# The plan of an attention kernel begins with VectorE and ScalarE still busy, and six small row transfers change their queue

## The chip, the cores and the metric

The kernel runs on one core of a Trainium2 chip. The metric is device time in microseconds (us) of one execution; the time before is the median of three. TensorE (PE in the profile) multiplies, VectorE (DVE), ScalarE (ACT) and GpSimd (POOL) work elementwise, SyncE (SP) issues most DMAs; ScalarE can issue DMAs from its own queue too.

## The reference

The input x has 2048 rows of 1024. Layer normalisation gives xn; an attention of 32 heads of 32 columns and a dense layer pair with Mish between (3584 wide) both read xn, and the output joins them.

```python
xn = _layernorm(x, axis=-1)
s = _A_ref(xn, A_wqkv, A_wo)
g = _silu(_B_ref(xn, B_w1, B_b1, B_w2))
return x + s * g
...
scores = jnp.einsum("bhqd,bhkd->bhqk", q, k) * (Dh ** -0.5)
p = _softmax(scores, axis=-1)
o = jnp.einsum("bhqk,bhkd->bhqd", p, v)
```

Everything is fp32. Products are made from a rounded high part and a low part each (three matmuls for one), which is why the code speaks of high and low, or of `THREE`.

## The kernel before, in words

There are four stages. In the first, x is normalised and transposed, and v is made for all heads. In the second ("qk"), 16 groups of 128 columns of q and k are made, four tiles of 512 rows each (`qk_group`, L626 is its matmul, in 24 steps); each tile leaves through ScalarE (high part), VectorE (low part) and a store issued from ScalarE's queue. The third is the plan, described below. The fourth finishes the output projection and writes the result.

Softmax needs the maximum of each row of scores before the exponentials. The kernel makes scores twice. First come the s tiles (queries on partitions, 128 by 512): VectorE takes the maximum of each (`mx`). Of 16 query tiles the 64 maxima go through a chain: reduce over the four key chunks and negate (`nm`), split into high and low (`hl`), turn by TensorE (`mtp`), copy by ScalarE (`mt`), and then two DMAs write them as rows 96 and 97 into the head's `qstack`, the right operand of the second pass. In the second pass the t tiles (keys on partitions, 512 queries each) come out with the maximum subtracted already, and ScalarE writes exp of them into `p`. A t tile of column block c (c = 0 to 3), called t(c=0) and so on, reads the 512 query columns of block c, rows 96 and 97 among them. GpSimd adds the p tiles up for the sum (`z`), TensorE multiplies them by v (`pv`).

For head 0, the s tiles and the first three quarters of the chain run already in the last four groups of the qk stage: `s_mm` (L553 matmul, L557 maximum) and, for every four query tiles, `m_tail` (groups g = 0, 1, 2, which become column blocks c = 0, 1, 2). The steps of `m_tail` are not issued at once but after 1, 2, 9 and 10 ticks of `Later`, a list that is run at the end of each tile and emptied when the stage ends. Group 0's rows so go out in the last qk tiles, those of groups 1 and 2 at the very end. The last four query tiles' maxima are finished inside the plan, by `m_chain(0, 12, 4, ...)`, and t(c=3) of head 0 waits for it (`m_there[0, 3]`); t(c=0) to t(c=2) of head 0 have no such entry in the planner's needs. The semaphores hold the real order in any case.

Within one engine's queue, instructions go in the order of the program. In the third stage that order is written by a planner (`Plan`, run once when the program is built). Five streams offer TensorE work: s of the next heads (L702), t (L785) with pv (L832), h (the first dense layer, L933, 24 matmuls for one tile), y (the second dense layer, L1022), and the output projection (L1119). Each matmul has a due time (`key`); the other engines' operations are added as their inputs are offered. The planner keeps a clock for each engine (`self.at`), gives each operation a fixed duration from the code, and takes from what is ready the one with the lowest key. Things that are limited are rings: seven PSUM banks `b`, two s tiles (`S_B`), two t tiles (`T_B`), and so on; an operation that takes from a ring waits, in the planner's time, until a place is given back. The planner's time decides only the order; the chip then runs it as semaphores allow.

All clocks of the planner begin at 0. The banks, which the qk stage still uses when the plan begins, have start times of their own:

```python
plan.rings["b"] = [(t, i) for i, t in enumerate((0.0, 0.2, 0.3, 0.9, 1.5, 2.1, 2.7))]
```

A DMA goes to SyncE's queue unless an engine is given:

```python
def move(out_, in_, eng=None):

    (eng or nc.sync).dma_start(out_.bitcast(F32), in_.bitcast(F32))
```

Of the kernel before, what the change touches and what calls it, by code (L numbers as in the profile page):

```python
# [18 lines left out]
P = 128  # L19
# [194 lines left out]
def body(ctx: ExitStack, tc: tile.TileContext, x, wqkv, wo, w1, b1, w2, out):  # L214
    nc = tc.nc
# [54 lines left out]
    def copy(out_, in_, scale=1.0):  # L270
        nc.scalar.activation(out_, in_, AF.Copy, scale=scale)  # L271

    def move(out_, in_, eng=None):

        (eng or nc.sync).dma_start(out_.bitcast(F32), in_.bitcast(F32))

    def low(eng, out_, in_, high):

        eng.tensor_tensor(out_, in_, high.bitcast(F32), ALU.subtract)  # L279
# [246 lines left out]
    def parts(i, n):  # L526
        return hls[i][:, :2 * n].rearrange("p (a b) -> p a b", a=2)

    def turn(tp, i):
        nc.tensor.matmul(tp[:, :P], hls[i], ident_r, start=True, stop=True)  # L530
# [30 lines left out]
    def m_tail(h, g, mx):  # L561
        nm = early.tile([P, NT], F32, tag=f"nm{g % 2}", name=f"nm{h}_{g}")[:, :4]
        hl = parts(g % 2, 4)
        mt = sp.tile([8, P], F32R, tag="mt", name=f"mt{h}_{g}")

        def r1():
            nc.vector.tensor_reduce(nm, mx[:, :4], axis=AX.X, op=ALU.max, negate=True)

        def r2():
            copy(hl[:, 0], nm)  # L570
            low(nc.vector, hl[:, 1], nm, hl[:, 0])

        def r3():
            tp = ps1.tile([P, 512], F32, tag="ps", name=f"mtp{h}_{g}")
            turn(tp, g % 2)
            copy(mt, tp[:8, :P])

        def r4():
            for a in range(2):
                move(qst[h % 3][96 + a:97 + a, g * 512:(g + 1) * 512]  # L580
                     .rearrange("o (t p) -> o t p", p=P), mt[4 * a:4 * a + 4, :])

        for t, fn in ((1, r1), (2, r2), (9, r3), (10, r4)):
            later.at(t, fn)
# [81 lines left out]
    plan = Plan()  # L666
# [6 lines left out]
    for i in (7, 6, 3, 1, 4, 2, 0, 5):  # L673
        ps_a.tile([P, 512], F32, tag=f"b{i}", name=f"free{i}")
    plan.rings["b"] = [(t, i) for i, t in enumerate((0.0, 0.2, 0.3, 0.9, 1.5, 2.1, 2.7))]

    def bank(at, name):
        return ps_a.tile([P, 512], F32, tag=f"b{at['b']}", name=name)
# [547 lines left out]
    for c in range(NC):  # L1226
        for s in range(4):
            t = 4 * c + s
# [49 lines left out]
```

## Time and profile before

| what | before |
|---|---|
| median of three runs | 3424.2 us (3423.58 to 3424.74) |
| the profiled execution's own time | 3424.24 us |
| its span in the trace | 3422.0 us |
| TensorE busy in the span | 3398.7 us |
| SyncE's queue, `qstack<-mt` issues in the whole span | 70 |

The span runs from the first to the last instruction of the program; the execution's own time is 2.2 us longer. Times in the trace are counted from the start of the span; the plan's first matmul is the s matmul at 577.53. A row of a timeline gives start, length, engine and line, what is written and read, how many instructions are merged into the row, and in brackets how long the engine stood idle ahead of it and what ended that. A q behind the engine's name (ACTq, SPq) is its queue issuing a DMA. Matmuls overlap, so that one that takes 0.39 us follows another 0.227 us later.

### The profile page before, as it was taken

Reading aid. Unit: us, or ns where it says so; the run is one execution under the profiler, and the core shown is the slowest. Engines: PE = TensorE matmul, PEld = TensorE weight load, DVE = VectorE, ACT = ScalarE, POOL = GpSimd, SP = SyncE. Lnnn points to the kernel's source line nnn. Section 1 sums busy time; section 2 is a strip of 40 time slices with the busy share of each in tenths; the row PEclk is TensorE's granted clock in tenths of the full one; section 3 lists DMA queues with packets and bytes.
Section 4 is the critical chain, followed back from the end, with each engine's and each line's share of the span. In section 5 each row is a group of like instructions: output and inputs, shape, how many; then the busy total and the mean of one; then the engine's idle time right before and its main releaser. Section 6 shows DMA issues by size and latency. Waiting matters only on the chain.

```text
span 3422.0 us, 47293 instructions
## 1 busy us (share of the span) xinstructions
PE 3398.7 (99%) x17827; PEld 2535.1 (74%) x17827; DVE 2326.9 (68%) x3750; ACT 1948.0 (57%) x3112; POOL 2461.5 (72%) x753
## 2 busy tenths in 40 slices
PE   8999999999999999999999999999999999999999
PEld 8998887677777767777677777777777677777687
DVE  6011236877878777788878787877878788876533
ACT  6111112766666667666666676666666666666621
POOL 0654342988888888888888888888888888888700
PEclk9999999999999999999999999999999999999999
DMA  8898897433334354343434443333445443333482
GB/s 289 288 309 303 292 314 241 124 111 100 118 105 124 105 167 136 111 120 103 124 99 124 149 148 111 112 117 107 126 113 183 123 121 112 112 117 119 140 290 85
DMA packets 294184, 529.71 MB, mean 155 GB/s; under 512 B 88810, under 2 KB 147178, under 8 KB 270186
## 3 DMA queue, kind: packets, MB, share of 16 engines
q1 hardware_dynamic: 274100, 484.74, 45.8%
q10 hardware_dynamic: 19856, 41.95, 3.3%
q8 instruction: 141, 2.31, 0.3%
q14 instruction: 87, 0.71, 0.1%
HBM read 386.89 MB, written 138.67 MB: 154 GB/s over the span
## 4 chain that ended last, share of the span: by engine, by line
PE 97%; DVE 2%; ACT 1%; DMA 0%; issue 0%; POOL 0%; DVEq 0%; POOLq 0%; ACTq 0%
PE y L1022 18%; PE h L933 17%; PE t L785 13%; PE pv L832 13%; PE s L702 13%; PE qk L626 10%; PE op L1119 5%; PE v L328 5%; DVE mx L708 1%; PE zp L858 1%; PE s L553 0%; PE pt L383 0%; ACT p L268 0%; DMA vraw<-in_A_wqkv_dram 0%; DVE st L355 0%
## 5 line engine op out<-in xcount | busy, mean ns | idle before, releaser
L814 POOL TENSOR_TENSOR z<-z,p 128x2048 f32<-128x2048 f32 x448 | 2066.2, 4612 | 192.0 <-ACT p L268 163.0
L268 ACT ACTIVATE p<-t,zero 128x512 f32<-128x512 f32 x2048 | 1385.3, 690 | 637.8 <-PE t L785 621.8
L708 DVE TENSOR_REDUCE mx<-s 128x1 f32<-128x512 f32 x1984 | 1327.8, 685 | 436.9 <-PE s L702 429.0
L1022 PE MATMUL y<-w,act 128*128 128x512 f32 x2688 | 937.7, 391 | 0.6 <-DVE yacc L1042 0.5
L785 PE MATMUL t<-qstack,kstack 128*128 128x512 f32 x2048 | 801.6, 393 | 0.9 <-DVE mx L708 0.6
L702 PE MATMUL s<-kstack,qstack 128*128 128x512 f32 x1984 | 779.4, 394 | 3.8 <-DVE mx L708 3.4
L933 PE MATMUL h<-xr,w 128*128 128x512 f32 x2016 | 715.2, 392 | 1.8 <-ACT act L271 1.8
L1022 PEld LDWEIGHTS y<-w,act 128*128 128x128 f32 x2688 | 503.0, 188 | 118.2 <-issue 8.4
L785 PEld LDWEIGHTS t<-qstack,kstack 128*128 128x128 f32 x2048 | 384.1, 188 | 110.4 <-issue 16.8
L702 PEld LDWEIGHTS s<-kstack,qstack 128*128 128x128 f32 x1984 | 371.3, 188 | 126.1 <-issue 24.3
L832 PE MATMUL pv<-p,v 128*32 128x512 f32 x4096 | 459.3, 594 | 0.0
L933 PEld LDWEIGHTS h<-xr,w 128*128 128x128 f32 x2016 | 378.9, 188 | 85.4 <-issue 5.0
L626 PE MATMUL qk<-xc,qkw 128*128 128x512 f32 x1536 | 350.9, 389 | 0.0
L814 POOL TENSOR_TENSOR z<-p,p 128x2048 f32<-128x2048 f32 x32 | 148.0, 4624 | 263.2 <-ACT p L268 182.2
L832 PEld LDWEIGHTS pv<-p,v 128*32 128x32 f32 x4096 | 123.3, 110 | 282.8 <-issue 282.1
L626 PEld LDWEIGHTS qk<-xc,qkw 128*128 128x128 f32 x1536 | 288.2, 188 | 59.8
L1042 DVE TENSOR_TENSOR yacc<-yacc,y 128x512 f32<-128x512 f32 x416 | 282.6, 679 | 52.3 <-PE y L1022 51.4
L933 PE MATMUL h<-xc,w 128*128 128x512 f32 x672 | 242.4, 391 | 0.1
L279 DVE TENSOR_TENSOR qst<-qk,qst 128x512 fp32r<-128x512 f32 x64 | 44.2, 691 | 246.0 <-ACT qst L271 246.0
L271 ACT ACTIVATE qst<-qk 128x512 fp32r<-128x512 f32 x64 | 38.3, 598 | 298.4 <-PE qk L626 262.1
L328 PE MATMUL v<-vw,xc 128*128 128x256 f32 x1536 | 191.1, 285 | 2.5 <-POOL vw L279 1.5
L328 PEld LDWEIGHTS v<-vw,xc 128*128 128x128 f32 x1536 | 186.9, 193 | 4.1 <-POOL vw L279 1.9
(91 smaller groups left out, 2273.7 us busy)
## 6 DMA issues: line engine op xcount, KB each, us to landing
w<-w1s SPq DMA_DIRECT2D x112, 1024.0 KB
w<-w2s SPq DMA_DIRECT2D x224, 512.0 KB
w2s<-pw SPq DMA_DIRECT2D x56, 512.0 KB
qstack<-qs SPq DMA_DIRECT2D x96, 256.0 KB
kstack<-ks SPq DMA_DIRECT2D x96, 256.0 KB
w1s<-w1p SPq DMA_DIRECT2D x20, 1024.0 KB
praw<-in_B_w_dram SPq DMA_DIRECT2D x72, 256.0 KB
x<-in_A_x_dram SPq DMA_DIRECT2D x32, 512.0 KB
```

The lines of the kernel that those rows point to most:

```text
L268: nc.scalar.activation(out_, in_, fn, bias=zero if bias is None else bias, scale=scale)
L328: nc.tensor.matmul(ps[:, :256], xc[t // 4][k // HK][:, a, k % HK, (t % 4) * P:(t % 4 + 1) * P], w[:, b, k], start=n == 0, stop=n == 3 * KT ...
L626: nc.tensor.matmul(ps, w[:, a, k], xc[c][k // HK][:, b, k % HK], start=n == 0, stop=n == 3 * KT - 1)
L702: nc.tensor.matmul(sp_, qst[h % 3][:, qt * P:(qt + 1) * P], kst[h % 3][:, kc * 512:(kc + 1) * 512], start=True, stop=True)
L708: nc.vector.reduce_max(tiles["mx"][:, qt, kc:kc + 1], tiles[qt, kc], axis=AX.X)
L785: nc.tensor.matmul(tp, kst[h % 3][:, kt * P:(kt + 1) * P], qst[h % 3][:, c * 512:(c + 1) * 512], start=True, stop=True)
L814: nc.gpsimd.tensor_tensor(zs[h], pts[T - 1] if kt == 1 else zs[h], pts[T], ALU.add)
L832: nc.tensor.matmul(pv[h][c * DH:(c + 1) * DH, :], vt[h][:, k, :], pts[T - kt + k][:, c * 512:(c + 1) * 512], start=k == 0, stop=k == NT - 1)
L933: nc.tensor.matmul(t["h"], w1t[n][:, a, k], xts_[c][k // HK][:, b, k % HK], start=i == 0, stop=i == 3 * KT - 1)
L1022: nc.tensor.matmul(t["y"], acts[n][:, p, s * P:(s + 1) * P], w2t[m_][:, q], start=j == 0 and i == 0, stop=j == YB - 1 and i == 2)
L1042: nc.vector.tensor_tensor(ya, ya, t["y"], ALU.add)
L1119: nc.tensor.matmul(ps[t, dh], ohl[t // 4, k][:, a, s * P:(s + 1) * P], wt[k][:, b, r], start=k == 0 and i == 0, stop=k == KT - 1 and i == 2)
```

## The change

Two edits. The planner's clocks of VectorE and ScalarE begin at 2.7 and 0.9 in place of 0. And the two row DMAs of each `m_tail` (six in all, 2 KB each) are issued from ScalarE's queue in place of SyncE's; those of `m_chain` stay where they are.

```diff
@@ -578,7 +578,7 @@
         def r4():
             for a in range(2):
                 move(qst[h % 3][96 + a:97 + a, g * 512:(g + 1) * 512]
-                     .rearrange("o (t p) -> o t p", p=P), mt[4 * a:4 * a + 4, :])
+                     .rearrange("o (t p) -> o t p", p=P), mt[4 * a:4 * a + 4, :], nc.scalar)
 
         for t, fn in ((1, r1), (2, r2), (9, r3), (10, r4)):
             later.at(t, fn)
@@ -673,6 +673,7 @@
     for i in (7, 6, 3, 1, 4, 2, 0, 5):
         ps_a.tile([P, 512], F32, tag=f"b{i}", name=f"free{i}")
     plan.rings["b"] = [(t, i) for i, t in enumerate((0.0, 0.2, 0.3, 0.9, 1.5, 2.1, 2.7))]
+    plan.at["DVE"], plan.at["ACT"] = 2.7, 0.9
 
     def bank(at, name):
         return ps_a.tile([P, 512], F32, tag=f"b{at['b']}", name=name)
```

## The prediction

> **What bounds the kernel now.** I read the page first, then busy time by stretches of the span, then the waits in three of these stretches, then the timeline of the microseconds in which the plan's instructions begin.
>
> ```profile
> span 3422.0 us, 47293 instructions
> PE 3398.7 (99%) x17827; PEld 2535.1 (74%) x17827; DVE 2326.9 (68%) x3750; ACT 1948.0 (57%) x3112; POOL 2461.5 (72%) x753
> PE 97%; DVE 2%; ACT 1%; DMA 0%; issue 0%; POOL 0%; DVEq 0%; POOLq 0%; ACTq 0%
> ```
>
> TensorE is busy for 3398.7 of 3422.0 us and makes 97% of the chain that ended last. A change that takes no matmul away can win at most the time in which TensorE stands still: 3422.0 - 3398.7 = 23.3 us. Busy time by stretches says how much of it lies where the plan rules.
>
> ```profile
> core 0: us, PE busy (x) PEld busy (x) DVE busy (x) ACT busy (x) POOL busy (x), PEclk, DMA share, GB/s
> 577.50:604.70 27.20, 24.70 (x107) 19.07 (x105) 26.08 (x43) 18.40 (x33) 12.36 (x3) 1.00 0.64 206
> 604.70:3200.00 2595.30, 2592.36 (x13490) 1839.43 (x13491) 2038.18 (x3237) 1737.59 (x2742) 2183.70 (x505) 1.00 0.41 121
> 3200.00:3245.00 45.00, 43.20 (x207) 32.06 (x206) 33.37 (x47) 28.34 (x43) 32.86 (x9) 0.96 0.49 165
> ```
>
> The plan's first matmul starts at 577.53 (shown below). In the 27.2 us from there TensorE is idle for 27.20 - 24.70 = 2.5 us, in the next 2595.3 us for 2.9 us, in the last 45 us for 1.8 us. The waits of TensorE, stretch by stretch (what waited, for whom, us in total, times, longest), name them:
>
> ```profile
> PE s L702 <- DVE mx L708: 1.9, 1, 1.9
> PE t L785 <- DVE mx L708: 0.6, 1, 0.6
> ...
> PE s L702 <- DVE mx L708: 1.5, 4, 0.5
> PE y L1022 <- DVE yacc L1042: 0.5, 1, 0.5
> PE y L1022 <- ACT p L268: 0.2, 1, 0.2
> PE t L785 <- ACT p L268: 0.2, 1, 0.2
> ...
> PE h L933 <- ACT act L271: 1.8, 1, 1.8
> ```
>
> The two ahead of the first "..." are the opening, the next four the long middle, the last the end. The opening in order of time, TensorE's rows first, then VectorE, ScalarE, SyncE:
>
> ```profile
> 577.53 0.91 PE L702 MATMUL s<-kstack,qstack 128*128 128x512 f32 x2
> 578.28 0.63 PE L933 MATMUL h<-xc,w 128*128 128x512 f32 x2
> 578.74 0.39 PE L785 MATMUL t<-qstack,kstack 128*128 128x512 f32 x1
> 578.97 0.39 PE L933 MATMUL h<-xc,w 128*128 128x512 f32 x1
> 581.23 0.50 PE L702 MATMUL s<-kstack,qstack 128*128 128x512 f32 x1 [1.86 <-DVE mx L708]
> ...
> 582.38 0.63 PE L785 MATMUL t<-qstack,kstack 128*128 128x512 f32 x2
> ...
> 588.15 0.47 PE L785 MATMUL t<-qstack,kstack 128*128 128x512 f32 x1 [0.58 <-DVE mx L708]
> ...
> 577.89 2.47 DVE L557 TENSOR_REDUCE mx<-s 128x1 f32<-128x512 f32 x4
> 580.40 0.17 DVE L722 TENSOR_REDUCE nm<-mx 128x4 f32<-128x16 f32 x1
> 580.49 0.68 DVE L708 TENSOR_REDUCE mx<-s 128x1 f32<-128x512 f32 x1
> ...
> 578.01 0.37 ACTq L275 DMA_DIRECT2D ks<-qst  x1
> 578.50 0.27 ACT L271 ACTIVATE mt<-mtp 8x128 fp32r<-8x128 f32 x1 [0.61 <-PE s L702]
> 580.61 0.21 ACT L271 ACTIVATE hl<-nm 128x4 fp32r<-128x4 f32 x1 [1.84 <-DVE nm L722]
> 580.72 0.67 ACT L268 ACTIVATE p<-t,zero 128x512 f32<-128x512 f32 x1
> ...
> 577.91 2.49 SPq L275 DMA_DIRECT2D qstack<-mt  x4
> 580.49 0.62 SPq L762 DMA_DIRECT2D v<-vs  x1
> 581.22 1.43 SPq L275 DMA_DIRECT2D w<-w1s  x1
> 582.74 1.21 SPq L275 DMA_DIRECT2D qstack<-mt  x2
> ```
>
> VectorE is still on the four last maxima of the stage ahead until 580.4, where the plan took it for free at once. Only two s tiles may be outstanding (S_B = 2), so the third s, seventh in TensorE's order (s s h h t h s), stands until the first maximum is out at 581.2: 1.86 us, with h matmuls ready behind it. That is what the first edit aims at. The 0.58 us at 588.15 is the same delay, carried on.
>
> **The change, part by part.** No instruction is added or removed; a start time in the planner and the queue of six small DMAs change.
>
> First, VectorE at 2.7 in the plan. The planner then places the third s after 2.7 + 0.69 = 3.4 in its own time, not near 1.3, and fills in with the 24 h matmuls that need nothing but loaded data. So both waits on VectorE, 1.86 + 0.58 = 2.44 us, go from where they are. What is late next? The t matmuls. By the rings in the code (bank times, two t tiles, MM 0.228) the order starts s s h h t h h, then comes t(c=1) where bank 1.5 is free, t(c=2) when the first exponential has given its t tile back: about 1.7 and 2.35 of the plan. These constants only order the work. On the chip, with plan zero at 577.46 and the 0.3 us that the first t already runs behind its place (0.98 of the plan, 578.74 on the chip), that is about 579.4 and 580.1. In the kernel before, both came at 582.38, behind the 1.86 us, so what they need was hidden; that cover is gone.
>
> Second, the rows. t(c=1) reads the rows of group 1 and t(c=2) those of group 2, each written by two DMAs, which the planner's needs don't hold. The four that SyncE issued at 577.91 now stand in ScalarE's queue: behind the store of 578.01, then two, then the second copy out of mtp (it stood at 578.50), then two. One of them costs
>
> ```profile
> L275 SPq DMA_DIRECT2D qstack<-mt x70: 565/576/1025, 552.4 to 3129.1; - x70
> ...
> GB/s 0 0 0 0 0 0 0 98 371 388 393 164 0 6 0 26 134 168 191 279 119 175 87 197 350 350 371 393 358 249 164 289 306 311 366 360 377 388 399 421
> ```
>
> 0.58 us of the queue's time (minimum, median, maximum in ns; 2.49 us for the four), on SyncE. ScalarE's price for it is not shown: its nearest row is 0.37 us for a store of another shape, the far end SyncE's 1.025. I take 0.58, the same transfer. The engine does not run ahead of its queue: the copy of 578.50 starts 0.12 us after the store's issue ends. So: 578.42 + 2 x 0.62 (issue and step) = 579.66; the copy with its start, 0.37, to 580.03; two more to 581.27; the first exponential 581.35 to 582.04.
>
> Landing: the lower row is what the DMA engines moved, in 40 slices of 0.375 us from 576.0. 98 to 164 GB/s, from 578.6 to 580.5, are the store of 578.01; the lone 6 in the slice from 580.9 to 581.25, 2 KB, is the last row transfer of before, whose issue began 3 x 0.62 = 1.87 us after 577.91, at 579.8. So about 1.3 us from issue to landing, and nothing before 580.5. Group 1 lands at 580.5 (issue of the second 579.05 + 1.3 = 580.35, held by the store), group 2 at 580.65 + 1.3 = 581.95. Hence t(c=1) waits from 579.4 to 580.55, 1.15 us; t(c=2) comes 0.7 us later, at 581.25, and waits to about 582.05 for both its rows and the exponential's tile: 0.8. Sum 1.95 us in place of 2.44.
>
> The rest hides. Rows of group 0, in the stage ahead, cost ScalarE 1.2 us there, in front of a 5.25 us idle time:
>
> ```profile
> 557.62 0.60 ACT L271 ACTIVATE qst<-qk 128x512 fp32r<-128x512 f32 x1 [5.25 <-PE qk L626]
> ```
>
> Without that idle time it would be the 1.2 us. On SyncE the v and w1 loads issue 2.5 us earlier, and h's second tile of weights with them; worth nothing while h has 24 matmuls in hand. The last four query tiles' rows (their copy hl now stands behind three exponentials, about 583.4, then rest, turn, copy and SyncE's two issues, 585.2 for the second) land near 586.5; t(c=3) has its place at 7.3 of the plan, 577.46 + 7.3 + 0.3 + 1.95 = 587.0. Hidden by 0.5 us; if that is gone, each 0.1 is 0.1.
>
> Sum against the profiled execution: 3424.24 us (span 3422.0 and 2.2 around it; the median of three is 3424.2) - 2.44 + 1.95 = 3423.75. **I predict 3423.7 us.**
>
> **The rivals.** *Faster: ScalarE's issues are short.* At 0.37 us (0.42 with its step) ScalarE is free at 580.45, the exponential done at 581.2, group 2 landed at 581.3: t(c=2) waits 0.1, the sum is 1.25, 1.2 less than before: 3423.0; with the store not in the way either, all 2.44: 3421.8. I put it at 3422.4. For it: 0.37 in ScalarE's queue; against it: that is another shape, and the 0.58 holds over 70 issues. The Trainium skill, "DMA: Bandwidth & Descriptors", section "Issuing engines are not separate DMA queues", calls the issue time usually small beside the DMA; that would be this rival, but here the issue, 0.58, is nearly half of the 1.3 from issue to landing.
>
> *Slower: the wait moves to ScalarE's queue and grows.* At 1.03 us an issue (1.08 with its step) group 1 lands at 580.8 (wait 1.4) and ScalarE is free at 583.1, so the exponential ends at 583.9 and t(c=2), due at 581.5, waits 2.4: 3.8 against 2.44, +1.4. A stop of that length can also slow TensorE afterwards, as at the end of the plan:
>
> ```profile
> 3198.42 5.83 PE L933 MATMUL h<-xr,w 128*128 128x512 f32 x25
> ...
> 3207.63 5.05 PE L933 MATMUL h<-xr,w 128*128 128x512 f32 x14 [1.80 <-ACT act L271]
> ```
>
> Here 25 h matmuls take 5.83 us, 0.227 apart; the 14 after the 1.80 us stop take 5.05, where 13 x 0.227 + 0.39 = 3.34 would do: 1.7 us more (granted clock 0.96 in that stretch). Together +3.1: 3427.3. It decides when t(c=2) starts after 582.55, half a microsecond later than I expect. Against it: the 1.86 us stop in the opening left the granted clock at 1.00. The Trainium skill, "TensorE: Matmul & The Clock Gate", section "Why this matters for your kernels", puts the drop at idle gaps of over about 3 us; by that this rival would be +1.4, 3425.6. The row of 1.80 us speaks against the figure.
>
> *The order after the opening is another.* The planner works each choice out from the last, so another opening may place later tiles otherwise. What it can win is what waits now: 1.5 + 0.5 + 0.2 + 0.2 in the middle and 1.8 + 1.7 at the end, 5.9 us: 3417.8. If the same comes a second time: 3429.6. Due times hold the order together (2.9 us idle in 2595), so I take it as a spread on both sides, more of it above: there are more places for a new wait than waits to lose.
>
> **How the numbers follow.** Forecast 0.43, own range 3422.7 to 3424.7; short issues 0.20; the growing wait 0.16; another order 0.21, of it 0.08 gains and 0.13 losses. The range 3420.0 to 3428.5 leaves out the outer parts of the last, some 0.04 below and 0.07 above, and little else. 0.2%, about what a measurement of this kernel can tell from no change, is 6.8 us. Faster by that (under 3417.4) needs nearly every wait from 577 on gone, 2.44 + 5.9 = 8.3: 0.03. Slower by that (over 3431.0) needs the growing wait and more than one further wait like the end's: 0.08. Within: 0.89.
>
> **What would show it.** Right: no wait of s on a maximum near 581; two waits of t between 579 and 582.2, on ScalarE or a DMA; in ScalarE's queue issues of qstack<-mt of 0.58 us, the first exponential at 581.3; SyncE's v issue near 578; idle time of the first 27 us still about 2 us. Wrong: exponentials before 580.5 (short issues), a t that starts after 582.55, or a busy time of TensorE in the middle or at the end that differs from 2592.36 and 43.20 by over 2 us (another order).

## The result, and the profile after

The changed kernel takes 3429.24 us (median of 17 runs), the kernel before on the same chips 3423.8 (17 runs): 1.0016 times as long, 95% interval 1.0009 to 1.0023. That is 5.4 us slower where I forecast no change that counts, and above the upper end of my range, 3428.5.

The page of the changed kernel, the three rows that answer to those of before:

```profile
span 3428.0 us, 47290 instructions
PE 3400.9 (99%) x17827; PEld 2535.6 (74%) x17827; DVE 2330.2 (68%) x3750; ACT 1948.4 (57%) x3112; POOL 2462.9 (72%) x753
PE 96%; DVE 2%; DMA 1%; ACT 0%; issue 0%; POOL 0%; SPq 0%; ACTq 0%; DVEq 0%; POOLq 0%
```

The work is the same and the span 6.0 us longer; a DMA is new in the chain that ended last. Its busy time by the same stretches (TensorE's clock is the column after POOL):

```profile
577.50:604.70 27.20, 23.32 (x94) 18.05 (x94) 21.28 (x37) 15.79 (x29) 9.58 (x3) 0.94 0.57 194
604.70:3200.00 2595.30, 2590.85 (x13470) 1837.40 (x13473) 2041.70 (x3240) 1735.54 (x2739) 2180.28 (x504) 1.00 0.41 121
3200.00:3245.00 45.00, 42.72 (x216) 31.26 (x209) 29.61 (x39) 29.66 (x46) 37.33 (x9) 1.00 0.51 169
```

In the first stretch TensorE does 94 matmuls in place of 107, at 0.227 us each some 3 us of work, and its clock is at 0.94. In the second it is idle for 1.5 us more than before (4.45 against 2.94). What TensorE waited for, ahead of the "..." to 605, then to 3200, then the end:

```profile
PE t L786 <- DMA qstack<-mt: 3.7, 1, 3.7
...
PE t L786 <- DMA qstack<-mt: 1.8, 1, 1.8
PE s L703 <- DVE mx L709: 0.6, 2, 0.5
PE t L786 <- ACT p L268: 0.5, 2, 0.3
...
PE h L934 <- ACT p L268: 2.3, 1, 2.3
```

Both waits of the opening on VectorE are gone. In their place a t matmul waits 3.7 us for a row transfer, and a second t waits 1.8 us for another. The opening in order of time (TensorE, ScalarE, SyncE):

```profile
578.39 0.39 PE L786 MATMUL t<-qstack,kstack 128*128 128x512 f32 x1
578.62 0.62 PE L934 MATMUL h<-xc,w 128*128 128x512 f32 x2
582.91 0.77 PE L786 MATMUL t<-qstack,kstack 128*128 128x512 f32 x1 [3.66 <-DMA qstack<-mt]
583.47 1.05 PE L934 MATMUL h<-xc,w 128*128 128x512 f32 x2
584.32 0.63 PE L786 MATMUL t<-qstack,kstack 128*128 128x512 f32 x1
584.75 1.80 PE L934 MATMUL h<-xc,w 128*128 128x512 f32 x5
...
577.66 0.37 ACTq L275 DMA_DIRECT2D ks<-qst  x1
578.12 1.48 ACTq L275 DMA_DIRECT2D qstack<-mt  x2
580.00 1.19 ACTq L275 DMA_DIRECT2D qstack<-mt  x2
581.23 0.69 ACT L268 ACTIVATE p<-t,zero 128x512 f32<-128x512 f32 x1 [1.27 <-DMA qstack<-mt]
...
563.61 0.58 SPq L763 DMA_DIRECT2D v<-vs  x1
576.30 0.33 SPq L275 DMA_DIRECT2D w<-w1s  x1
587.85 1.44 SPq L275 DMA_DIRECT2D qstack<-mt  x2
```

The t at 582.91 is t(c=1). The nine matmuls from there to 586.39 take 3.48 us, some 1.4 us more than at 0.227 us each. ScalarE's queue is nearly as forecast: 0.58 us for three of the four row transfers and 0.86 for the other, first exponential at 581.23. SyncE's is not: with the rows gone from it, v went out at 563.6 (580.49 before) and the 1 MB load of h's second weight tile, w, at 576.30 (581.22 before), as soon as the last qk tile was done (its weights had the buffer). The DMA queues show what that did. Packets, MB and share of the 16 engines' time by queue (q1 is SyncE's, q10 ScalarE's), changed kernel, from 578.6 to 580.6 and from 580.6 to 583:

```profile
q1 hardware_dynamic: 87, 0.71, 102.5%
...
q10 hardware_dynamic: 304, 0.53, 57.9%
q1 hardware_dynamic: 24, 0.07, 8.3%
```

and the kernel before, from 578.6 to 580.6:

```profile
q10 hardware_dynamic: 272, 0.52, 70.2%
q1 hardware_dynamic: 24, 0.01, 1.4%
```

Before, the last q/k store (0.52 MB, issued at 578.01) had the DMA engines nearly to itself in these two microseconds. After, they carry the load alone, not one packet of the store, which was issued at 577.66; the store moves behind the load, and the rows behind the store. So t(c=1) has group 1's rows at 582.91, where I had forecast 580.5.

The second wait is in the planner's order. SyncE's queue ahead of head 1's first t, before and after:

```profile
648.29 1.21 SPq L275 DMA_DIRECT2D qstack<-mt  x2
649.59 0.58 SPq L762 DMA_DIRECT2D v<-vs  x1
650.26 1.01 SPq L275 DMA_DIRECT2D qstack<-zeros  x1
```
```profile
652.14 1.27 SPq L275 DMA_DIRECT2D qstack<-zeros  x1
...
656.19 1.21 SPq L275 DMA_DIRECT2D qstack<-mt  x2
...
663.37 0.47 PE L786 MATMUL t<-qstack,kstack 128*128 128x512 f32 x1 [1.82 <-DMA qstack<-mt]
...
664.44 0.63 PE L1023 MATMUL y<-w,act 128*128 128x512 f32 x1
...
667.00 0.63 PE L703 MATMUL s<-kstack,qstack 128*128 128x512 f32 x1
```

Before, head 1's rows went out ahead of the loads of head 3 (they begin with zeros); now they stand behind six of them, 1.5 MB, and the t at 663.37 waits. From 664.44 on, eight matmuls start 0.43 us apart (the rows at 664.44 and 667.00 are two of them), not 0.227.

Of the 6.0 us between the two spans I can place most: the opening is 13 matmuls (3.0 us) behind at 604.7, though it began 0.35 earlier; head 1 costs 1.8 + 7 x 0.2 = 3.2; the end gives back 1.2 (wait 2.3 for 1.8, but none of the 1.7 us of slow matmuls). The rest, about 1 us, lies in short waits that I did not trace one by one.

### The profile page after: what moved, and what is told of

Its sections match the earlier page's. It is cut to its first block, busy times and chain, and to the rows that moved or that the text cites. A ratio compares the mean times of both kernels' runs of the same rounds, so it can differ in the third digit from the quotient of the medians.

```text
span 3428.0 us, 47290 instructions
## 1 busy us (share of the span) xinstructions
PE 3400.9 (99%) x17827; PEld 2535.6 (74%) x17827; DVE 2330.2 (68%) x3750; ACT 1948.4 (57%) x3112; POOL 2462.9 (72%) x753
## 4 chain that ended last, share of the span: by engine, by line
PE 96%; DVE 2%; DMA 1%; ACT 0%; issue 0%; POOL 0%; SPq 0%; ACTq 0%; DVEq 0%; POOLq 0%
PE y L1023 18%; PE h L934 17%; PE t L786 13%; PE pv L833 13%; PE s L703 13%; PE qk L626 10%; PE op L1120 5%; PE v L328 5%; PE zp L859 1%; DVE mx L709 1%; PE s L553 0%; DMA qstack<-mt 0%; PE pt L383 0%; ACT p L268 0%; DVE st L355 0%
```

## The experiments

Runs of one kernel spread by some microseconds, mostly upward (before: 3423.02 to 3429.31), so differences under about 1.5 us are not told apart by medians; for those I go by the traces. "Above before" is against the runs of before on the same chip; the changed kernel is 5.4 above.

My theory after the result: the freed SyncE let the 1 MB load go out 5 us earlier, and it holds up the store and the rows behind it. Rivals: ScalarE's four issues hold t; the planner's new order alone is the loss.

**Only the start times** (rows on SyncE):

```diff
-                     .rearrange("o (t p) -> o t p", p=P), mt[4 * a:4 * a + 4, :], nc.scalar)
+                     .rearrange("o (t p) -> o t p", p=P), mt[4 * a:4 * a + 4, :])
```

> The planner's start times alone; the rows of groups 1 and 2 go out from SyncE as before the change, so that v and the 1 MB load of h's second weights stand behind them. TensorE's, VectorE's and GpSimd's orders are the changed kernel's. Theory (the freed SyncE let the 1 MB load go out 5 us earlier, ahead of the store and the rows): the load issues near 580.9 again, the store moves from 578.6, the rows land by 580.5 to 581.2, t(c=1) starts near 580.5 and not at 582.9, no slow matmuls follow; the stop of 1.8 at 663 (head 1's rows behind head 3's loads on SyncE) stays, since it is in the planner's order. 2.4 + 1.2 us less than the changed kernel: about 3425.5. Rival (the planner's order alone is the loss): opening and total as in the changed kernel, about 3429. Second rival (ScalarE's four issues hold t): the same time as the theory here, so this run does not tell these two apart.

3424.86 against 3423.22: 1.6 above before (1.0005, 0.9996 to 1.0014). SyncE issues the rows from 577.80, the load at 581.11:

```profile
581.02 0.47 PE L786 MATMUL t<-qstack,kstack 128*128 128x512 f32 x1 [1.52 <-DMA qstack<-mt]
```

t(c=1) starts at 581.02, no slow matmuls follow, and the stop at head 1 stays (1.9 us near 661). A second stop of 1.30 us stands at 588.37, where t(c=3) waits for its own rows. So the same order on TensorE costs 3.8 us less with the rows on SyncE. The order alone is not the loss.

**Only the queue** (the line with 2.7 and 0.9 taken out):

```diff
-    plan.at["DVE"], plan.at["ACT"] = 2.7, 0.9
```

> The rows from ScalarE's queue, the planner's clocks at 0, so the order of before. Theory: the 1 MB load goes out near 576.3 and the rows land near 582.6 as in the changed kernel; t(c=1), which came at 582.38 before, waits some 0.3 to 0.5 us; ScalarE's hl comes 0.7 later than before; no stop near 663, as in before. About 3424.5 to 3425.5. Rival (ScalarE's issues alone are the loss): the third s still waits to 581.2, then t(c=1) and the exponentials stand longer, 3426 or more with the load wherever it is. Rival (the planner's order alone): 3423.8, as before.

3424.27 against 3423.22: 1.05 above before. The load goes out at 576.58, the rows are late, but the old order asks for t(c=1) only behind the third s, which still waits 1.85 us for VectorE. What I had not expected: after that stop six matmuls run slowly, so that t(c=1), at 583.64, finds its rows. Alone, each edit's loss (1.6 and 1.05 us) is at the edge of what the medians tell; together it is 5.4.

**The 1 MB load behind the rows**, everything else as in the changed kernel:

```diff
-        move(w1t[n], w1s[n % FT])
+        move(w1t[n], w1s[n % FT], nc.scalar if n == 1 else None)
```

> The changed kernel, but the 1 MB load of h's second weight tile is issued from ScalarE's queue, where it stands behind the rows (one issue of 0.35 us more ahead of the first exponential). TensorE's, VectorE's and GpSimd's orders are the changed kernel's. Theory: the store moves from 578.3 to 580.2, group 1's rows land near 580.5 and group 2's near 582, t(c=1) starts near 580.5 in place of 582.9, the opening stop is 1.2 to 2 us and no slow matmuls follow; the stop at 663 stays. About 3425.5 to 3426.5. Rival (ScalarE's issues hold t): t(c=1) still starts after 582 and the time is 3429 or more, because ScalarE has one issue more. Rival (the planner's order): 3429.

3424.53 against 3423.22: 1.3 above before, 4.1 less than the change. ScalarE issues the load at 581.18, behind the rows. From 578.5 to 580.5 the store has the engines:

```profile
q10 hardware_dynamic: 288, 0.53, 70.5%
```

and t waits about as long as the prediction had it:

```profile
580.99 0.47 PE L786 MATMUL t<-qstack,kstack 128*128 128x512 f32 x1 [1.53 <-DMA qstack<-mt]
581.29 0.63 PE L934 MATMUL h<-xc,w 128*128 128x512 f32 x2
582.32 0.47 PE L786 MATMUL t<-qstack,kstack 128*128 128x512 f32 x1 [0.39 <-DMA qstack<-mt]
```

1.53 + 0.39 = 1.92 us; I had worked out 1.95, for a kernel in which the load does not go out early. That the sums agree so closely is partly luck: my two waits were 1.15 and 0.8, and t(c=1) comes 0.44 us later than I had it. (The time is a microsecond under what I expected of it: the stop at head 1 is only 1.0 us here.) The order of the instructions on TensorE, VectorE and GpSimd is the changed kernel's, ScalarE has one issue more, and 4 us are gone. By the traces about 3 us of the difference lie in the opening (1.74 of waits and 1.4 of slow matmuls) and the rest mostly at head 1. In the opening it is the load's place, not ScalarE's issues.

**Head 3's loads behind head 1's rows**:

```diff
-        loaded[h] = op("SP", 0.5, need=[last_t[h - 3]] if h >= 3 else [], ...
+        loaded[h] = op("SP", 0.5, need=[last_t[h - 3], m_there.get((h - 2, 3))] if h >= 3 else [], ...
```

> The changed kernel, but a head's loads are not planned before the rows of the head two ahead of it are out (head 3's after head 1's rows). Theory: the opening is as in the changed kernel (t(c=1) at 582.9, 3.7 us), but the stop of 1.8 at 663 and the seven slow matmuls behind it are gone: 3.2 less, about 3426. If the stop at 663 comes from something else (GpSimd's place for head 1's low part), it stays and the time is 3429.

3427.0 against 3423.22: 3.8 above before, 1.6 less than the change, half of what I expected. The stop on the DMA at head 1 is gone (0.3 us on ScalarE is left). But after the opening's stop of 3.67 us twelve matmuls ran slowly, where the changed kernel had six, with a loss of 1.4 us in all; that ate 1 us or more.

**The store from SyncE, ahead of the load**, so that the rows have ScalarE's queue to themselves:

```diff
-        later.at(1, lambda: move(dst, st, nc.scalar))
+        later.at(1, lambda: move(dst, st, None if f == 2 * KT - 1 and c == 0 else nc.scalar))
```

> The changed kernel, but the last q/k store goes out from SyncE, ahead of the 1 MB load in that queue, so that the rows have ScalarE's queue to themselves and the load stands behind the store. TensorE's, VectorE's and GpSimd's orders are the changed kernel's. Theory (rows wait because the store ahead of them in their own queue waits for the load's packets): store 578.6 to 580.2, the load's packets only after it, group 1's rows land near 580.3, t(c=1) starts near 580.4; opening stop 1 to 1.5 us, no slow matmuls; stop near 660 stays. About 1.3 above before: 3424.5. Rival (a loaded set of DMA engines holds small transfers whatever their queue): rows wait for the load's end as well, t(c=1) after 582.5, 3428 or more.

3427.62 against 3423.95: 3.7 above before (1.0009, 1.0000 to 1.0017). My theory of the queue falls here. With nothing ahead of them in their own queue and the load behind the store, the rows still waited:

```profile
582.04 0.47 PE L786 MATMUL t<-qstack,kstack 128*128 128x512 f32 x1 [2.61 <-DMA qstack<-mt]
```

By queue, from 578.6 to 580.4 and from 580.4 to 582.6:

```profile
q1 hardware_dynamic: 254, 0.52, 92.9%
...
q1 hardware_dynamic: 2098, 0.40, 123.0%
q10 hardware_dynamic: 32, 0.01, 1.7%
```

The store and then v, which is 2048 packets, both on SyncE's queue, keep the engines; the rows on ScalarE's, issued from 577.74, get through only from 580.4 on, in between v's packets: eight of their 32 packets pass in each of the stretches from 580.4, 580.9, 581.4 and 582.0. The other forecast is not met in full either, as t(c=1) starts at 582.04 and not after 582.5. So a small transfer can be held by what the DMA engines have under way, from whichever queue: the store held the rows wholly, v in part. In the changed kernel that was the load, then the store.

**The planner told that the rows are late**, DMAs as in the changed kernel:

```diff
-    plan.at["DVE"], plan.at["ACT"] = 2.7, 0.9
+    plan.at["DVE"], plan.at["ACT"] = 2.7, 3.7
...
+    for c, when in ((1, 5.5), (2, 5.6)):
+        m_there[0, c] = Op("SP", 0.0)
+        m_there[0, c].end = when
```

> The changed kernel with its DMAs as they are, but the planner is told when the rows are there: t(c=1) not before 5.5 and t(c=2) not before 5.6 of the plan, and ScalarE busy to 3.7. It then puts ten more h matmuls and the s matmuls ahead of t(c=1). Theory (the loss is that nothing else stood ahead of a late transfer): rows still land near 582.6, but TensorE hardly stops in the opening (under 0.5 us), no slow matmuls; a stop near 660 may stay. 2.4 to 3 us less in the opening than before, 1.8 to 3.2 more at 660: 3422 to 3424. Rival (the 1 MB load in front costs by itself, through the DMA engines): the opening still stops for over 2 us, 3427 or more.

3423.96 against 3423.95: as before. The load goes out at 576.61 and the rows as late as in the change, but TensorE has eleven h matmuls and more ahead of t(c=1):

```profile
578.94 2.69 PE L934 MATMUL h<-xc,w 128*128 128x512 f32 x11
581.47 0.39 PE L703 MATMUL s<-kstack,qstack 128*128 128x512 f32 x1
...
583.40 0.39 PE L786 MATMUL t<-qstack,kstack 128*128 128x512 f32 x1
```

No stop stands in the opening, early load or not: what costs there is a t placed where its rows have not landed, with nothing ahead of it. That the early load costs nothing at all is not shown. The time is only as before, though the 2.44 us of stops in the opening of before are gone, and the last run below, with the load behind the rows and other landings told, is 3.4 below before; what parts the two was not traced.

**The same with the rows on SyncE**, landings told as 3.5 and 3.6, ScalarE's clock at 1.2, and the edit of head 3's loads:

> Rows from SyncE as before, the planner told of their landing (3.5 and 3.6) and ScalarE busy to 1.2, a head's loads planned behind the rows of the head two ahead. Theory: no stop at t(c=1) or t(c=2); up to 1.2 at t(c=3), whose rows stand behind the 1 MB load on SyncE; none near 660. 2 to 3 less than before: 3420.5 to 3421.5. If later waits grow by the new order, up to 3424.

3425.35 against 3423.95 (its runs from 3423.53 to 3432.02, the traced one 3431.09): a miss. t(c=1) and t(c=2) do not wait, but t(c=3) does, twice as long as I had allowed: its rows were issued at 582.55, behind the load of 580.75 in the same queue.

```profile
587.60 0.47 PE L786 MATMUL t<-qstack,kstack 128*128 128x512 f32 x1 [2.41 <-DMA qstack<-mt]
```

**Rows from ScalarE with the load behind them, landings told as 3.4 and 4.7, ScalarE's clock at 4.1, head 3's loads behind head 1's rows**:

> All of it: rows from ScalarE with the 1 MB load behind them in the same queue, the planner told of the landings (3.4 and 4.7) and ScalarE busy to 4.1, a head's loads planned behind the rows of the head two ahead. Theory: under 0.5 us of stops in the opening, no slow matmuls, none near 660: 2.5 to 3.3 less than before, 3420 to 3421. If the exponentials, which begin at 581.7, then hold t: a stop of 1 us at t(c=2) or t(c=3) and 3422.

3419.58 against 3423.95: 4.4 below before (0.999, 0.9981 to 0.9999), 9.8 below the change by the two differences. Its busy time in the stretches 577.5 to 600 and 600 to 700, and below it the same two rows of the changed kernel:

```profile
577.50:600.00 22.50, 22.42 (x95) 17.08 (x94) 21.87 (x38) 14.93 (x28) 7.60 (x2) 1.00 0.70 253
600.00:700.00 100.00, 100.00 (x530) 69.30 (x529) 85.69 (x135) 71.74 (x116) 92.36 (x22) 1.00 0.41 113
```
```profile
577.50:600.00 22.50, 18.70 (x75) 14.68 (x75) 16.58 (x29) 11.25 (x21) 4.96 (x2) 0.92 0.59 204
600.00:700.00 100.00, 97.49 (x506) 66.13 (x505) 81.67 (x127) 68.54 (x110) 85.76 (x20) 0.98 0.38 102
```

TensorE does not stand still from the second s to 700 us.

Two more runs part the last two edits. **The load behind the rows and head 3's loads later**, with nothing told:

> The 1 MB load behind the rows on ScalarE (as in e3) and head 3's loads planned behind head 1's rows (as in e4), the planner told of nothing else. Its orders on TensorE, VectorE and GpSimd are those of e4. Theory (two costs that add): opening stops of 1.9 as in e3, the stop of head 1's t that e3 still had (1.1) gone, no slow matmuls: 1 to 1.3 us less than e3, so about 0.2 above before, 3424. Rival (the stop at head 1 comes from the late opening and only hides a matmul that waits elsewhere): as e3, 1.3 above before.

3424.62 against 3424.18: 0.4 above before. Opening stops of 1.9, none at head 1 on a DMA, as expected; the trace shows 0.7 us of short waits near 681 in its place, so the gain over the run without that edit is not settled. **The fastest version without the edit of head 3's loads**:

> The version that was 4.4 us under before, without the edit of head 3's loads. Theory: the opening has no stops either way; what the edit is worth is a stop of t of head 1 near 655, 1 to 2 us, if the planner again puts head 1's rows behind head 3's loads, and nothing if it doesn't. 3419.5 to 3422, under before in any case. If the opening needs that edit, 3423 or more.

3420.77 against 3424.18: 3.4 below before (0.999, 0.9981 to 0.9999). One stop of 0.9 us on head 1's rows is left. Most of the gain is the opening's.

## Why the prediction was wrong

Point by point:

- *Both waits on VectorE go, 2.44 us:* right; no s waits on a maximum before 605.
- *t(c=1) and t(c=2) come at 579.4 and 580.1 and are uncovered:* right; TensorE came to t(c=1) at 579.25, and it was the next thing late.
- *ScalarE's issue 0.58 us, exponential at 581.35:* right but for one issue of 0.86; 581.23, in an opening that began 0.35 us earlier. The rival of short issues is out.
- *"Group 1 lands at 580.5, group 2 at 581.95":* wrong, and this is the step that failed. It took the DMA engines' load from the trace of before, though a paragraph later I moved SyncE's loads: *"On SyncE the v and w1 loads issue 2.5 us earlier ...; worth nothing while h has 24 matmuls in hand"*. I asked what the earlier load would win and not what it would stand in front of. The w1 load issued not 2.5 but 4.9 us earlier, since in before it had waited behind v and the rows, and those in turn behind their copies (v, for which I had named 578 as a sign, went out at 563.61); the load then moved 0.71 MB in the two microseconds in which I had the store move. The opening's waits became 3.66 us, not 1.95. With the load put behind the rows, the third experiment measured 1.92, split otherwise than I had it.
- *Slow matmuls after a stop, 1.7 us, only in the rival:* they came, 1.4 us in the opening and 1.4 at head 1.
- *The slower rival, 3427.3, decided by t(c=2) later than 582.55:* the sign of its case (t(c=2) at 584.32, then slow matmuls) was there, but its cause was not ScalarE's queue. I gave it 0.16.
- *Another order, a spread on both sides:* one place was the loss, head 1's rows behind head 3's loads, 3.2 us by the trace. My sign for it, TensorE's busy time in the middle or at the end off by over 2 us, did not show it: 1.5 and 0.5, because slow matmuls count as busy. It was to be had from the code only by working out the plan as far as 650 us, but it could have been named as a place: one queue holds both the rows that the next t needs and 1.5 MB that it does not need.

The Trainium skill, "DMA: Bandwidth & Descriptors", section "Issuing engines are not separate DMA queues", says that DMAs of all issuing engines run on the same 16 DMA engines. The store's run agrees: a t waited 2.61 us for rows alone in ScalarE's queue, which got through only when the store from SyncE was done. The Trainium skill, "DMA: Bandwidth & Descriptors", section "Queues, rings and completion order", has each DMA engine take turns between queues, a packet at a time, and a packet there is typically some 9 to 17 descriptors, drained whole. The traces do not decide it. From 578.6 to 580.6 the load on q1 passed 87 packets of the profile and the store on q10, issued at 577.66, none; but by an estimate from 0.71 MB in 87 and 0.52 MB in 254, the load is some 128 and the store some 256 of them, 8 and 16 for each of 16 engines. If these are the page's descriptors, each may have passed in one turn. The rows that passed between v's packets fit the taking of turns.

## What to carry to other kernels

Where a small transfer leaves a queue, ask what comes out of that queue sooner and in front of what: what the DMA engines have under way can hold a later small transfer, whichever queue it came from. Here one early megabyte held the 2 KB rows that a matmul needs for some two microseconds (t(c=1) at 582.91 with the load in front, at 580.99 with it behind). A planner that orders instructions for an engine that is 99% busy should be told of every transfer that an instruction needs: telling it two landings, and how long ScalarE is busy, brought the whole loss back with the DMAs untouched. When a wait is taken away, list what the next instructions in that queue need and whether the old wait had covered it.

## What the runs showed of the hardware that I had not expected

After a stop TensorE sometimes ran at half its rate for some matmuls, and the length of the stop did not decide it. Stops of 1.85 us (queue alone), 1.82 (head 1 in the change) and 3.66 were followed by six, eight and six matmuls 0.43 us apart, 3.67 by twelve; those of 1.86 in the opening of before, 1.52 in the first experiment and 2.6 at the end of the fastest version by none.

The granted clock in the traces says more. Each of these slow stretches is a step of 3.41 us at a clock of 0.50 (two steps in a row after the 3.67), and in the 3.41 us just ahead of the stretch TensorE had stood idle for at least 1.8 us. Four rows of the kernel before, with the clock behind POOL: the last is the slow step at the end of the plan and the third what is ahead of it; the first two are the opening, in steps counted back from that one:

```profile
576.98:580.39 3.41, 2.38 (x11) 1.40 (x9) 3.08 (x5) 0.81 (x3) 0.00 (x0) 1.00 0.42 155
580.39:583.81 3.42, 2.58 (x12) 2.13 (x13) 3.28 (x7) 2.04 (x5) 0.00 (x0) 1.00 0.70 102
3205.25:3208.66 3.41, 1.61 (x8) 1.04 (x7) 2.28 (x4) 3.41 (x7) 3.41 (x1) 1.00 0.87 301
3208.66:3212.07 3.41, 3.41 (x10) 2.64 (x9) 2.00 (x4) 1.43 (x3) 3.33 (x2) 0.50 0.90 320
```

Ahead of the slow step TensorE was idle for 3.41 - 1.61 = 1.80 us. The 1.86 us of the opening fall across two steps, 1.03 and 0.84, and no slow one follows. The step ahead was idle for 3.15 and 1.82 us in the change and for 2.30 in the run with 3.67. So it seems to matter where a stop falls on these steps, and that may differ from one execution to the next. It is not the whole rule: in the first experiment, in steps counted back from a slow one at the very end of its trace, the step from 3206.31 was idle for 1.89 us and no slow one followed.
